# Every value product of an attention stage as two products of 64 rows, in two PSUM banks, added up by VectorE

## The chip, the cores and the metric

The kernel runs on one core of a Trainium2 chip. The metric is the device time of one execution in microseconds (us), the median of several runs. A profiled execution gives, beside its own time, a span: from its first to its last instruction.

The core's engines have short names in the profile: PE is TensorE's products (matmuls), PEld its loads of the stationary operand, DVE is VectorE, ACT is ScalarE, POOL is GpSimd, SP is SyncE, which here issues the DMA transfers. TensorE writes to PSUM, eight banks of 128 partitions x 512 f32 values; VectorE and ScalarE read them.

## The reference

```python
xn = layernorm(x)                                   # x: 2048 x 576
q, k, v = split(xn @ wqkv)                          # 32 heads of 18
p = softmax(q @ k.T * 18 ** -0.5)                   # 2048 x 2048 per head
s = (p @ v, heads joined) @ wo
g = silu((gelu(xn @ w_gate) * (xn @ w_up)) @ w_down)  # 4608 hidden values
out = x + s * g
```

## The kernel before, in words

After a prologue that normalizes x and computes q, k and v, the kernel runs attention and the feed-forward block side by side. Attention works on 32 units u (8 groups of four heads, times 4 blocks of 512 query tokens); a unit has 16 key tiles kt of 128 tokens. The feed-forward block works on sections of 128 hidden values for 512 tokens. The order on TensorE is written out by hand; the other engines' instructions are ordered by the scheduler, apart from those kept in program order.

`section` (L533) issues 27 pairs of products pg and pu (L413), one on the partitions 0 to 63 and one on 64 to 127, and mixes 16 further pairs in: of each, one is a score product pe (`score_mm`, L729) and one a product pm for a later unit's score maxima (`max_mm`, L698). Each pm takes a bank of tag m, of which there are three (`BANKS`), and VectorE reduces it to its row maxima (L699). Each pe takes a bank of tag s, and ScalarE makes the exponentials pT from it (L730). The pg and pu banks have tag f.

The loop at L829 goes through 128 attention sections, four per unit (i = 0 to 3). After every odd one it issues a value stage: `values` (L755) for eight key tiles. For each key tile and each of the four heads a, one product multiplies the values VS (128 key tokens x 32 columns, of which 19 count: ones for the softmax's sum and the 18 values) with the exponentials pT (128 key tokens x 512 queries). It accumulates over the eight key tiles in the partitions 32a to 32a + 31 of one bank acc of tag m. After the first stage of a unit ScalarE copies acc to the SBUF tile SUM (L767); after the second VectorE adds acc to SUM (L769), and DMAs store the sums (L772 and `store_sums`, L605). So 64 value stages alternate between the two kinds of eviction. VS and pT are f32, and the trace has two instructions per product.

After every even attention section `downs` (L573) issues the down products py (L465), 48 pairs of 64 rows x 288 columns in banks of the tags m, s and f, whose sums VectorE adds to Y (L453); VectorE also does the feed-forward's elementwise work (L427, L434, L440), and GpSimd the splits of weights and hidden values.

The section behind a value stage begins with a pair pg/pu; its first score pair comes second, and its first pm needs a bank of tag m again. Banks of a tag are handed out in turn.

Of the kernel before, what the change touches and what calls it, by code (L numbers as in the profile page):

```python
# [8 lines left out]
F32 = mybir.dt.float32  # L9
F32R = mybir.dt.float32r  # L10
AF = mybir.ActivationFunctionType
ALU = mybir.AluOpType
# [5 lines left out]
P = 128  # L18
NT = S // P
TB = 512  # L20
# [3 lines left out]
HR = 64  # L24
# [9 lines left out]
NA = NS // SLOTS  # L34
VC = NT // NA
VV = 2 * VC
KB, VB = 7, 2
# [32 lines left out]
def kernel(ctx: ExitStack, tc: tile.TileContext, x, wqkv, wo, w_gate, w_up, w_down, out):  # L70
    nc = tc.nc
# [85 lines left out]
    with tc.tile_pool(name="pro", bufs=1) as pro, tc.tile_pool(name="pps", bufs=1, space=PSUM) as pps:  # L157
# [45 lines left out]
        def norm(xr, b, between=None, behind=None):  # L203
            keep = tc.keep_in_program_order if b == 1 else lambda i: i
            st = pro.tile([P, 4, 8], F32, name="st", bufs=2)
            for j in range(4):
                bs = pro.tile([P, 2, 6], F32, name="bs", bufs=2)
                for h in range(2):
                    one = nc.vector.bn_stats(bs[:, h, :], xr[j][:, 288 * h:288 * h + 288])  # L209
                    keep(one)  # L210
                if behind and j == 0:
                    behind(one)
                nc.vector.bn_aggr(st[:, j, 0:2], bs)
            var, r, t = st[:, :, 1], st[:, :, 3], st[:, :, 4]
            nc.scalar.activation(t, var, AF.Sqrt, bias=eps)
            if between:
                between()
            nc.vector.reciprocal(r, t)
            nc.vector.scalar_tensor_tensor(t, r, -0.5, r, op0=ALU.mult, op1=ALU.mult)
            nc.vector.scalar_tensor_tensor(t, var, EPS, t, op0=ALU.add, op1=ALU.mult)  # L220
            nc.vector.scalar_tensor_tensor(r, t, 1.5, r, op0=ALU.add, op1=ALU.mult)
            for j in range(4):
                last = nc.vector.tensor_scalar(xr[j][:, 0:D], xr[j][:, 0:D], st[:, j, 0:1], st[:, j, 3:4],
                                               op0=ALU.subtract, op1=ALU.mult)
                nc.scalar.activation(xr[j][:, D:D + HR], xr[j][:, R0:D], AF.Copy)
            return last
# [42 lines left out]
        def split_qk(t, raw):  # L269
            hi, lo = (pro.tile([P, KT, P], F32R, name=f"q{m}{t}") for m in "hl")  # L270
            first = split(hi, lo, raw)
            put_qk(t, hi, lo)
            return first
# [62 lines left out]
        last = norm(xr, 0, first_hi, first_loads)  # L336
# [10 lines left out]
        for b in range(NB):  # L347
            for n, t in enumerate(ORDER):
                if n == (2 if b == 0 else 0) and b + 1 < NB:
                    xr = load_x(b + 1)  # L350
                if b == 0 and ahead_qk:
                    first = split_qk(*ahead_qk.pop(0))
# [34 lines left out]
    ps = ctx.enter_context(tc.tile_pool(name="ps", bufs=1, space=PSUM, reuse_waits="tile"))  # L387
# [213 lines left out]
    def store_sums(g, cols):  # L601

        for a in range(QD):
            h = QD * g + a
            kept(nc.sync.dma_start(oT[h * DH:(h + 1) * DH, cols], SUM[32 * a + 1:32 * a + 1 + DH, :]))  # L605
# [7 lines left out]
    def at(n, part, what, *args):  # L613
        todo.setdefault((n, part), []).append(lambda: what(*args))
# [10 lines left out]
    SUM = key.tile([P, TB], F32, name="accs")  # L625
# [19 lines left out]
    with tc.tile_pool(name="att", bufs=1, reuse_waits="tile") as att:  # L645
        VS = [att.tile([P, VC * VW + 32 - DH - 1], F32, name=f"VS{i}") for i in range(VB)]
# [28 lines left out]
        QS, MX, ACC, PT, DEN, PIECE = {}, {}, {}, {}, {}, {}  # L675
# [79 lines left out]
        def values(u, kt):  # L755
            j, g = divmod(u, NQ)
            first, last = kt % VV == 0, kt % VV == VV - 1
            if first:
                ACC[u] = ps.tile([P, TB], F32, name="acc", tag="m", bufs=3)
            pt = PT.pop((u, kt))  # L760
            for a in range(QD):
                c, t = divmod(kt, VC)
                v = t * VW + (DH + 1) * a
                nc.tensor.matmul(ACC[u][32 * a:32 * a + 32, :], VS[(u * NA + c) % VB][:, v:v + 32], pt[:, a, :],  # L764
                                 start=first, stop=last, skip_group_check=True)
            if last and kt < VV:
                nc.scalar.activation(SUM, ACC.pop(u), AF.Copy)  # L767
            elif last:
                nc.vector.tensor_tensor(SUM, ACC.pop(u), SUM, op=ALU.add)  # L769
            if kt == NT - 1 and u < NU - 1:  # L770
                cols = slice(j * TB, (j + 1) * TB)
                nc.sync.dma_start(sT[QD * g:QD * (g + 1), cols], SUM.rearrange("(a p) t -> a p t", p=32)[:, 0, :])  # L772
                store_sums(g, cols)
                rt = rT[QD * g:QD * (g + 1), cols]
                todo.setdefault(((u + 1) * NA, 0), []).insert(0, lambda: sums(u, rt))
                at((u + 1) * NA + 2, 2, reciprocals, u, rt)
                for h in range(2 if u < NU - 2 else 0):
                    at((u + 1) * NA + 3 + h, 2 * h, load_piece, u, h)
                    at((u + 1) * NA + 4 + h, 2 * h, norm_piece, u, h)
# [10 lines left out]
        def sums(u, rt):  # L790
            j, g = divmod(u, NQ)
            den = DEN[u] = att.tile([P, QD * TB // P], F32, name="sums", bufs=2)
            nc.sync.dma_start(den, sT[QD * g:QD * (g + 1), j * TB:(j + 1) * TB]
                              .rearrange("a (c s) -> a c s", s=QD * TB // P))
# [34 lines left out]
        for n in range(NU * NA):  # L829
            u, i = divmod(n, NA)  # L830
            s0 = n * SLOTS
            new_x = (FF["n"] + 1) % (NR * G) == 0
            if new_x:
                load_k(n - 1 + KB, behind_it)
            section([p for s in range(s0, s0 + SLOTS) for p in slot_pairs(s)])
            if n > 0 and not new_x:
                load_k(n - 1 + KB)
            if n > NU * NA - KB:
                load_wo((n - 1) % KB)
            if i == 1 and u + 2 < NU:  # L840
                load_q(u + 2)
            tasks(n, 0)
            um, im = divmod(s0 + LEAD + SLOTS, NS)
            if im == 0 and um <= NU:
                max_neg(um - 1)
                at(n + 1, 0, max_rows, um - 1)
            if i % 2:
                for kt in range((i - 1) * VC, (i + 1) * VC):
                    values(u, kt)
                load_v(n + 1)  # L850
                load_v(n + 2)
            downs()
            tasks(n, 2)
            finish()


    with tc.tile_pool(name="epi", bufs=1, reuse_waits="tile") as epi:
# [80 lines left out]
        for n in range(NU * NA, ENDS):  # L938
            first, last = n == NU * NA, n == ENDS - 1
# [102 lines left out]
```

## Time and profile before

| | |
|---|---|
| median of 3 runs | 2548.01 us (2547.96 to 2548.17) |
| the profiled execution | 2547.22 us |
| its span | 2545.4 us |
| granted TensorE clock | 1.000 |
| value products (L764), busy | 452.8 us, 4096 instructions |
| reduces of the maxima (L699), busy | 1249.6 us, 2048 instructions |
| exponentials (L730), busy | 1153.3 us, 2048 instructions |
| 1190.00 to 1223.25 us, two sections with a value and a down stage: DVE, ACT, POOL busy | 27.19, 22.96, 17.15 us of 33.25 |

A row of the timeline gives the start, the length, the engine, the line, the operation, output<-input, the shape (rows*columns of the stationary operand, then the moving operand), and how many instructions are merged in it (x4); in brackets the engine's idle time before it and what ended that. A product's length goes to the end of its last result, so products that follow each other overlap in the rows, and the distance of starts shows the pace. A row of groups ends with busy time in us, mean ns of one, idle time before, and what ended it. A row of waits has the total in us, how often, and the longest.

### The profile page before, as it was taken

What the parts mean: (1) busy time and instruction counts of PE and PEld (TensorE: products, weight loads), DVE (VectorE), ACT (ScalarE), POOL (GpSimd) and SP (SyncE); (2) the same over time, 40 slices, a digit from 0 to 9 for tenths busy, and PEclk for the clock granted to TensorE, in tenths of its full rate; (3) what the DMA queues carried; (4) which work ended last, traced back from release to release, by engine and by line L of the source; (5) the groups of instructions that cost most, each with busy time, mean ns of one, the idle gap of its engine ahead of it and who ended that gap; (6) DMA issues with size and microseconds to landing.
All of it is one profiled execution on the core that took longest, in us unless ns stands there. A gap on an engine that the chain in (4) does not pass through costs nothing.

```text
span 2545.4 us, 63167 instructions
## 1 busy us (share of the span) xinstructions
PE 2538.4 (100%) x23974; PEld 2008.4 (79%) x23974; DVE 1950.4 (77%) x3499; ACT 1555.1 (61%) x3050; POOL 1320.7 (52%) x1447
## 2 busy tenths in 40 slices
PE   9999999999999999999999999999999999999999
PEld 8888877777777777777777787777777777787798
DVE  5316988888888888888888888888888888887277
ACT  3223366666677666676666677666676666676612
POOL 2117545555465554445565545554446555455675
PEclk9999999999999999999999999999999999999999
DMA  8876444444465444444455444444446444444483
GB/s 267 269 241 158 100 103 106 100 111 109 107 150 121 104 109 112 113 112 110 111 125 140 116 111 106 105 108 112 109 109 153 115 109 109 108 106 99 114 242 107
DMA packets 398686, 325.51 MB, mean 128 GB/s; under 512 B 117408, under 2 KB 309184, under 8 KB 398384
## 3 DMA queue, kind: packets, MB, share of 16 engines
q1 hardware_dynamic: 398384, 321.47, 49.7%
q8 instruction: 191, 3.13, 0.5%
q14 instruction: 111, 0.91, 0.1%
HBM read 266.63 MB, written 54.70 MB: 126 GB/s over the span
## 4 chain that ended last, share of the span: by engine, by line
PE 98%; ACT 1%; DVE 0%; DMA 0%; SPq 0%; issue 0%; ACTq 0%
PE pg L413 29%; PE py L465 18%; PE acc L764 18%; PE pm L698 9%; PE pe L729 9%; PE po L180 7%; PE pu L413 6%; PE po L902 2%; ACT pT L730 1%; PE pt L241 0%; SPq L665 0%; DMA xx<-in_A_x_dram 0%; DVE bs L209 0%; ACT t L426 0%; DMA KS<-qk 0%
## 5 line engine op out<-in xcount | busy, mean ns | idle before, releaser
L730 ACT ACTIVATE pT<-pe 128x512 f32<-128x512 f32 x2048 | 1153.3, 598 | 368.7 <-PE pm L698 226.3
L699 DVE TENSOR_REDUCE mx<-pm 128x1 f32<-128x512 f32 x2048 | 1249.6, 680 | 151.3 <-PE pm L698 149.0
L413 PE MATMUL pg<-xd,wh 64*128 64x512 f32 x2592 | 928.9, 390 | 0.0
L413 PE MATMUL pu<-xd,wh 64*128 64x512 f32 x2592 | 928.6, 390 | 0.0
L698 PE MATMUL pm<-KS,q 64*128 64x512 f32 x2048 | 779.0, 388 | 0.8 <-DMA KS<-qk 0.5
L729 PE MATMUL pe<-q,KS 64*128 64x512 f32 x2048 | 775.2, 387 | 0.0
L413 PEld LDWEIGHTS pg<-xd,wh 64*128 64x128 f32 x2592 | 476.5, 184 | 115.9 <-POOL wh L106 21.1
L413 PE MATMUL pg<-xd,wl 64*128 64x512 f32 x1296 | 501.6, 387 | 0.0
L413 PE MATMUL pu<-xd,wl 64*128 64x512 f32 x1296 | 501.4, 387 | 0.0
L413 PEld LDWEIGHTS pu<-xd,wh 64*128 64x128 f32 x2592 | 477.0, 184 | 2.0
L764 PE MATMUL acc<-pT,VS 128*32 128x512 f32 x4096 | 452.8, 594 | 0.0
L108 POOL TENSOR_TENSOR wl<-raw,wh 128x384 fp32r<-128x384 f32 x432 | 434.2, 1019 | 13.7
L106 POOL TENSOR_SCALAR hh<-t 128x512 fp32r<-128x512 f32 x128 | 79.1, 618 | 652.0 <-DVE t L440 637.8
L698 PEld LDWEIGHTS pm<-KS,q 64*128 64x128 f32 x2048 | 374.2, 184 | 31.1 <-DVE mx L699 4.3
L729 PEld LDWEIGHTS pe<-q,KS 64*128 64x128 f32 x2048 | 370.9, 184 | 21.9
L465 PE MATMUL py<-dh,hh 64*128 64x288 f32 (+1 forms) x2160 | 360.3, 294 | 0.3
L465 PE MATMUL py<-dl,hh 64*128 64x288 f32 (+1 forms) x2160 | 358.7, 292 | 0.0
L465 PE MATMUL py<-dh,hl 64*128 64x288 f32 (+1 forms) x2160 | 358.3, 292 | 0.0
L764 PEld LDWEIGHTS acc<-pT,VS 128*32 128x32 f32 x4096 | 127.4, 110 | 289.9 <-issue 278.0
L106 POOL TENSOR_SCALAR wh<-raw 128x384 fp32r<-128x384 f32 x432 | 217.2, 515 | 143.7 <-PE pu L413 83.4
L453 DVE TENSOR_TENSOR Y<-py,Y 128x288 f32<-128x288 f32 x544 | 227.1, 452 | 59.8 <-PE py L465 52.7
L413 PEld LDWEIGHTS pg<-xd,wl 64*128 64x128 f32 x1296 | 238.7, 184 | 32.1
(119 smaller groups left out, 3106.7 us busy)
## 6 DMA issues: line engine op xcount, KB each, us to landing
KS<-qk SPq DMA_DIRECT2D x1536, 36.0 KB
raw<-in_B_w_gate_dram SPq DMA_DIRECT2D x144, 288.0 KB
raw<-in_B_w_up_dram SPq DMA_DIRECT2D x144, 288.0 KB
raw<-in_B_w_down_dram SPq DMA_DIRECT2D x67, 576.0 KB
VS<-vs SPq DMA_DIRECT2D x128, 152.0 KB
qk<-t SPq DMA_DIRECT2D x72, 256.0 KB
q<-qk SPq DMA_DIRECT2D x384, 36.0 KB
xx<-in_A_x_dram SPq DMA_DIRECT2D x32, 288.0 KB
```

The source lines that it names most:

```text
L106: first = nc.gpsimd.tensor_scalar(hi, raw, 1.0, 1.0, op0=ALU.mult, op1=ALU.mult)
L108: low_part[:] = [keep(nc.gpsimd.tensor_tensor(lo, raw, f(hi), op=ALU.subtract))]
L180: nc.tensor.matmul(o, st, m, start=(i == 0), stop=(i == len(terms) - 1))
L413: nc.tensor.matmul(o, w[1 + wp][k][rr, c, :], xd[xp][k][rr, c, :], start=(i == 0), stop=(i == len(terms) - 1))
L453: one = kept(nc.vector.tensor_tensor(yy, py, yy, op=ALU.add))
L465: return nc.tensor.matmul(py, hs[g][a][rr, j * P:(j + 1) * P], wd[w][rr, g, 288 * c:288 * c + 288], start=start, stop=stop)
L698: nc.tensor.matmul(pm, QS[u, r][rr, t * P:(t + 1) * P], KS[(u * NA + c) % KB][r][rr, :], start=True, stop=True)
L699: nc.vector.tensor_reduce(MX[u][:, 2 * r + a, t, c:c + 1], pm, axis=AX.X, op=ALU.max)
L729: nc.tensor.matmul(pe, KS[(u * NA + c) % KB][r][rr, t * P:(t + 1) * P], QS[u, r][rr, :], start=True, stop=True)
L730: nc.scalar.activation(PT[u, kt][:, 2 * r + a, :], pe, AF.Exp, scale=SCALE)
L764: nc.tensor.matmul(ACC[u][32 * a:32 * a + 32, :], VS[(u * NA + c) % VB][:, v:v + 32], pt[:, a, :], start=first, stop=last, skip_group_chec ...
L902: nc.tensor.matmul(po, parts_of(b, j)[x_][:, k, :], OW[w][c][k], start=(i == 0), stop=(i == len(OUT) - 1))
```

## The change

A value product is issued as two, one for each half of the 128 key tokens (partitions 0 to 63 and 64 to 127); the halves h accumulate in two banks acc of tag m, both held for the whole stage. At the end the first half is evicted as before (by ScalarE after a unit's first stage, by VectorE after its second), and the second half is added to SUM by VectorE.

```diff
             if first:
-                ACC[u] = ps.tile([P, TB], F32, name="acc", tag="m", bufs=3)
+                ACC[u] = [ps.tile([P, TB], F32, name="acc", tag="m", bufs=3) for h in range(2)]
             pt = PT.pop((u, kt))
             for a in range(QD):
                 c, t = divmod(kt, VC)
                 v = t * VW + (DH + 1) * a
-                nc.tensor.matmul(ACC[u][32 * a:32 * a + 32, :], VS[(u * NA + c) % VB][:, v:v + 32], pt[:, a, :],
-                                 start=first, stop=last, skip_group_check=True)
-            if last and kt < VV:
-                nc.scalar.activation(SUM, ACC.pop(u), AF.Copy)
-            elif last:
-                nc.vector.tensor_tensor(SUM, ACC.pop(u), SUM, op=ALU.add)
+                for h in range(2):
+                    rr = slice(HR * h, HR * h + HR)
+                    nc.tensor.matmul(ACC[u][h][32 * a:32 * a + 32, :], VS[(u * NA + c) % VB][rr, v:v + 32], pt[rr, a, :],
+                                     start=first, stop=last, skip_group_check=True)
+            if last:
+                for h, acc in enumerate(ACC.pop(u)):
+                    if h == 0 and kt < VV:
+                        nc.scalar.activation(SUM, acc, AF.Copy)
+                    else:
+                        nc.vector.tensor_tensor(SUM, acc, SUM, op=ALU.add)
```

## The prediction

> **What bounds the kernel now.** I read the busy times, the chain that ended last, TensorE's waits and the costliest groups.
>
> ```profile
> PE 2538.4 (100%) x23974; PEld 2008.4 (79%) x23974; DVE 1950.4 (77%) x3499; ACT 1555.1 (61%) x3050; POOL 1320.7 (52%) x1447
> PE 98%; ACT 1%; DVE 0%; DMA 0%; SPq 0%; issue 0%; ACTq 0%
> PE pm L698 <- DMA KS<-qk: 0.5, 1, 0.5
> L699 DVE TENSOR_REDUCE mx<-pm x2048: 625/679/693, 212.9 to 2336.4; 128x1 f32<-128x512 f32 x187
> L764 PE MATMUL acc<-pT,VS x4096: 592/592/618, 324.3 to 2417.0; 128*32 128x512 f32 x196
> ```
>
> TensorE (PE) is on the chain for 98% of the span, and the longest wait that is listed for its products from the first score product on is 0.5 us. So time is won or lost only by what TensorE streams, by what lies between two streams, and by new waits. The value products (L764) are 4096 instructions: 64 stages of 64, that is 8 key tiles, 4 heads, and two instructions per product (the tile is plain f32). VectorE (DVE) is 77% busy as an average, but that average misleads. Here are the stage that starts at 1190.70 and its loads:
>
> ```profile
> 1190.38 0.39 PE L413 MATMUL pu<-xd,wh 64*128 64x512 f32 x1
> 1190.70 0.64 PE L764 MATMUL acc<-pT,VS 128*32 128x512 f32 x4
> 1190.70 0.16 PEld L764 LDWEIGHTS acc<-pT,VS 128*32 128x32 f32 x8 [0.35 <-issue]
> 1191.15 0.13 PEld L764 LDWEIGHTS acc<-pT,VS 128*32 128x32 f32 x4 [0.30 <-issue]
> 1191.58 0.13 PEld L764 LDWEIGHTS acc<-pT,VS 128*32 128x32 f32 x4 [0.30 <-issue]
> 1196.73 1.04 PE L764 MATMUL acc<-pT,VS 128*32 128x512 f32 x8
> 1197.70 0.50 PE L413 MATMUL pg<-xd,wh 64*128 64x512 f32 x1
> 1198.04 0.39 PE L698 MATMUL pm<-KS,q 64*128 64x512 f32 x1
> 1198.27 0.39 PE L413 MATMUL pg<-xd,wl 64*128 64x512 f32 x1
> ```
>
> The reader is to see three things. Four value products, one per head in its own 32 columns, run side by side, and a round of four takes 0.43 us (1191.15 to 1191.58): 16 rounds, 6.88 us. Around the stage, pairs of 64-row products come every 0.23 us (1198.04 to 1198.27). And both ends cost extra. Entry: 1190.38 to 1191.15 is 0.77 where 0.23 + 0.43 would do, 0.11 too much. Exit: the last round starts near 1196.73 + 1.04 - 0.59 = 1197.18; from there to 1198.04 is 0.86, where 0.43 + 0.23 would do, 0.20 too much. Together 0.31 us per stage.
>
> VectorE's reduces of the score maxima come at the pace at which TensorE makes them:
>
> ```profile
> 1185.37 6.07 DVE L699 TENSOR_REDUCE mx<-pm 128x1 f32<-128x512 f32 x10
> 1219.33 5.46 DVE L699 TENSOR_REDUCE mx<-pm 128x1 f32<-128x512 f32 x9
> 1223.95 0.64 PE L764 MATMUL acc<-pT,VS 128*32 128x512 f32 x4
> 1215.20 1.22 DVE L699 TENSOR_REDUCE mx<-pm 128x1 f32<-128x512 f32 x2
> 1215.88 0.18 PEld L698 LDWEIGHTS pm<-KS,q 64*128 64x128 f32 x1
> ```
>
> Ten back to back take 6.07 us: one each (6.07 - 0.68)/9 = 0.60 us, so 16 of a section need 9.6 us, and its 43 pairs (27 for gate and up, 16 with scores) 43 x 0.226 = 9.7 us. VectorE has next to no slack there, and the three PSUM banks of tag m tie it to TensorE. The last two rows show how tightly: the first of the two reduces ends at 1215.20 + 0.63 = 1215.83 and the load that needs its bank starts at 1215.88, 0.05 us later.
>
> **The change part by part.**
>
> *Streams.* Each product becomes two of 64 rows: 128 instructions and 128 loads a stage instead of 64 and 64. Four column tiles side by side are shown above; two row tiles side by side are the pg/pu pairs. Both at once is in no row. If eight run side by side, and the length goes by the 512 columns of f32 and not by the rows, a round stays 0.43 us. The eight loads at 1190.70 start within 0.16 - 0.11 = 0.05 us, 7 ns apart; four more streams put the last one 0.03 us later, 64 x 0.03 = **+1.9 us**. Bounds: below, the 64-row products around the stage need 0.23 us per 512 columns, half of 0.43, so at most -0.20 x 16 x 64 = -205 us; above, the halves run one after the other, +6.88 x 64 = +440 us. I take the value next to the rows for four columns and two rows, no change of pace.
>
> *The two ends.* The change keeps 64 rows throughout, so only the columns differ from the neighbours'. Whether that saves the 0.31 us (64 x 0.31 = 20 us) is answered by the one place where the trace changes the columns alone, 128 rows before and after:
>
> ```profile
> 329.87 1.47 PE L764 MATMUL acc<-pT,VS 128*32 128x512 f32 x12
> 331.27 0.40 PE L465 MATMUL py<-dh,hh 128*128 128x288 f32 x1
> 331.51 0.30 PE L465 MATMUL py<-dl,hh 128*128 128x288 f32 x1
> 331.64 0.29 PE L465 MATMUL py<-dh,hl 128*128 128x288 f32 x1
> ```
>
> The last round starts at 329.87 + 1.47 - 0.59 = 330.75, ends its 0.43 at 331.18, and the next product comes at 331.27, 0.09 late; the one behind it after 0.24 where 0.13 is the pace. 0.20 us again, as at 1197.70, where rows and columns both change. I take **0**, and keep -20 us as the other end.
>
> *The second bank at the entry.* Tag m has three banks. The last three score products of a section hold them; before, acc took the oldest. Now the second instruction of the stage needs the bank of the last product but one. At 1190.70 the reduces end at 1185.37 + 6.07 = 1191.44, the last but one at 1190.84; with 0.05 for the release the load can start at 1190.89, 0.19 after 1190.70. At 1223.95: 1219.33 + 5.46 = 1224.79, 1224.19, 1224.24, so 0.29. These two kinds of stage alternate. Behind the waiting load stand all the stage's other products; I take it that they wait with it, so the stage ends that much later. The reduces end at 2336.4 and stages come every 33.25 us (1190.70 to 1223.95) from 324.3 on: 61 have this wait. 61 x 0.24 = **+14.6 us**. Nothing below 0 is to be had here; above, if TensorE stood still until the last reduce, 0.6 us more each, +37.
>
> *The second eviction at the exit.* There is one more add of 0.69 us on VectorE per stage, in front of the next section's 16 reduces.
>
> ```profile
> 1197.92 0.60 ACT L767 ACTIVATE accs<-acc 128x512 f32<-128x512 f32 x1 [4.84 <-DMA KS<-qk]
> 1198.50 3.87 DVE L699 TENSOR_REDUCE mx<-pm 128x1 f32<-128x512 f32 x6 [4.69 <-PE pm L698]
> 1199.21 0.18 PEld L698 LDWEIGHTS pm<-KS,q 64*128 64x128 f32 x1
> 1199.66 0.18 PEld L698 LDWEIGHTS pm<-KS,q 64*128 64x128 f32 x1
> 1231.17 0.69 DVE L769 TENSOR_TENSOR accs<-acc,accs 128x512 f32<-128x512 f32 x1 [4.14 <-PE acc L764]
> 1231.78 4.44 DVE L699 TENSOR_REDUCE mx<-pm 128x1 f32<-128x512 f32 x7
> 1232.91 0.18 PEld L698 LDWEIGHTS pm<-KS,q 64*128 64x128 f32 x1
> 1234.40 0.56 SPq L772 DMA_DIRECT2D sT<-accs  x1
> L453 DVE TENSOR_TENSOR Y<-py,Y 128x288 f32<-128x288 f32 x544 | 227.1, 452 | 59.8 <-PE py L465 52.7
> ```
>
> First kind: ScalarE (ACT) copies half 0 until 1198.52, the add starts at 1198.57, the reduces 0.61 later at 1199.18 instead of 1198.50. The fourth score product takes the bank of the first reduce, free at 1199.18 + 0.68 + 0.05 = 1199.91; its load stood at 1199.66: 0.25 late. Second kind: adds at 1231.17 and 1231.78, first reduce at 1232.39, bank free at 1233.12 against 1232.91: 0.21 late. VectorE runs no faster than TensorE in the section, so this isn't won back by TensorE; what is left of VectorE's own delay (some 0.4 us) goes into its waits for finished sums in the down products (L453: 52.7 us, 0.8 per stage). 61 x 0.23 = **+14.0 us**. The store of the sums (L772) stood at 1234.40, far behind the second add's end at 1232.47, so SyncE's queue hides its delay; without that cover what stands behind it there (the key and query loads) would go 0.6 us later, once in every second stage. Bounds: 0 if VectorE's slack took it all; if VectorE is given the first reduce ahead of the add in the first kind, the second bank comes free at 1199.11 + 0.69 + 0.05 = 1199.85, and its load (third score product, at 1199.21) is 0.64 late: 0.39 x 31 = 12 us more.
>
> *Sum.* 1.9 + 0 + 14.6 + 14.0 = 30.5 us. The profiled execution took 2547.2 us (span 2545.4), 0.8 under the median of 2548.0. 2548.0 + 30.5 = 2578.5; I say 2578.
>
> **The rivals.**
>
> *TensorE can't be fed.* 128 products and 128 loads in 6.88 us are one instruction in 27 ns. The densest run is that of the down products:
>
> ```profile
> 1208.50 0.30 PE L465 MATMUL py<-dl,hh 64*128 64x288 f32 x2
> 1208.64 0.29 PE L465 MATMUL py<-dh,hl 64*128 64x288 f32 x2
> ```
>
> Two products (and two loads) in 0.13 us, 66 ns per product. If that is a ceiling, a stage takes 128 x 0.066 = 8.4 us, 1.5 more, +98 us; with the exit's 14 it ends near 2660. Against it: 128-row products come every 0.13 us too (331.51 to 331.64) with half the instructions, so 0.13 is the stream's length and no limit of issue. [...] Chance 0.12 (2610 to 2680).
>
> *The halves take turns:* +440 us and up, near 3000. Against it, row pairs and column fours each run side by side. 0.05.
>
> *The ends are spared.* Decided where the tile changes: if 64 rows kept means nothing extra there, -20 us. It is faster only if the waits at the banks, 28.6 us by the rows, come to under half of that sum as well; otherwise the reduces, not the ends, set when the stage starts, and it falls back towards the forecast: 2558 if the saving comes off whole. 0.07 for 2525 to 2543, 0.06 for 2543 to 2553.
>
> *A 64-row f32 stream runs at the 64-row pace.* This is the case on the faster side in one mechanism: place L764, price up to -205 us, about 2370; it decides once a round falls by 0.03 us (16 x 0.03 outweighs 0.48 of waits). Against it: the neighbours are another number format (one instruction per product, not two). 0.04.
>
> **How the numbers follow.** Forecast 0.66, own range 2560 to 2592 (one of the two waits missing, or the ends spared and swallowed by the waits; the reduce ahead of the add). The range of 2548 to 2670 takes in that, half of the case within 0.2%, and nearly all of the feeding limit: 0.66 + 0.03 + 0.11 = 0.8. Under 0.2% (5 us) is no difference that a measurement can tell. Faster 0.11, same 0.06, slower 0.83.
>
> **What would show it.** Right: rounds of eight still 0.43 us apart; first value load still 0.3 us behind the last pair, the second 0.2 to 0.3 us later; 32 + 64 adds of 0.69 us; the reduces after a stage 0.6 to 0.7 us later; periods of 33.7 instead of 33.25. Wrong: rounds longer or shorter than 0.43, products evenly spaced instead of in eights, or a stage whose first two loads start together.

## The result and the profile after

The changed kernel takes 2584.1 us (median of 4 runs, 2583.7 to 2584.3) against 2548.0 of the kernel before: ratio 1.0142, 95% interval 1.013 to 1.0155. It is slower by 36 us, where 30.5 were forecast. The profiled execution's span went from 2545.4 to 2582.3 us, 36.9 more. From the profile's page (busy times, the chain, and two groups):

```profile
PE 2575.0 (100%) x28070; PEld 2205.1 (85%) x28070; DVE 1978.9 (77%) x3563; ACT 1566.4 (61%) x3050; POOL 1320.4 (51%) x1447
PE 98%; ACT 1%; DVE 1%; DMA 0%; SPq 0%; issue 0%; DVEq 0%; ACTq 0%
L766 PE MATMUL acc<-pT,VS 64*32 64x512 f32 x8192 | 468.6, 591 | 0.0
L773 DVE TENSOR_TENSOR accs<-acc,accs 128x512 f32<-128x512 f32 x96 | 66.4, 692 | 298.5 <-PE acc L766 139.2
```

The page hides the cause: TensorE is as "busy" as before. The waits, 0.1 to 0.3 us each, lie under products that are still in flight, and a product whose load comes late is listed longer (0.47 us against 0.39, in rows below). The trace has to be cut where the work changes. I cut each of the 63 periods from one value stage to the next at the starts of TensorE's rows: the first value product, the first pg behind it, the first down product, the first product behind the last down product. Sums over the 63 periods, in us:

| | before | after | difference |
|---|---|---|---|
| value stage, to the next pg | 441.3 | 457.0 | +15.6 |
| the section behind it | 609.1 | 623.1 | +13.9 |
| down products | 417.5 | 422.1 | +4.6 |
| the next section, to the next stage | 618.3 | 620.3 | +2.0 |
| sum | 2086.2 | 2122.4 | +36.2 |

The line between the last two parts is soft, because in some periods the next section's first products come among the last down products: cut at that section's first product, and not behind the last down product, the two differences are +5.6 and +1.1. Their sum stays.

**The stage's start.** The loads and the reduces at one stage in the changed kernel:

```profile
1240.06 0.13 PEld L766 LDWEIGHTS acc<-pT,VS 64*32 64x32 f32 x2 [0.35 <-DVE mx L699]
1240.36 0.27 PEld L766 LDWEIGHTS acc<-pT,VS 64*32 64x32 f32 x15 [0.16 <-DVE mx L699]
1240.81 0.24 PEld L766 LDWEIGHTS acc<-pT,VS 64*32 64x32 f32 x8 [0.19 <-issue]
1238.43 2.47 DVE L699 TENSOR_REDUCE mx<-pm 128x1 f32<-128x512 f32 x4
```

Two loads (head 0, half 0) start, and the next comes 0.30 us behind the first. The four reduces end at 1238.43 + 2.47 = 1240.90, the last but one at 1240.30, and the second half's load follows at 1240.36: it waits for the second bank. The rest wait behind it. In the other kind of stage the gap is 0.17 us; these are its loads, then its first and last products and what follows:

```profile
1206.27 0.14 PEld L766 LDWEIGHTS acc<-pT,VS 64*32 64x32 f32 x2 [0.35 <-issue]
1206.45 0.18 PEld L766 LDWEIGHTS acc<-pT,VS 64*32 64x32 f32 x14
...
1205.96 0.39 PE L413 MATMUL pu<-xd,wh 64*128 64x512 f32 x1
1206.28 1.69 PE L766 MATMUL acc<-pT,VS 64*32 64x512 f32 x24
...
1212.05 1.49 PE L766 MATMUL acc<-pT,VS 64*32 64x512 f32 x23
1213.47 0.49 PE L413 MATMUL pg<-xd,wh 64*128 64x512 f32 x1
1213.81 0.39 PE L698 MATMUL pm<-KS,q 64*128 64x512 f32 x1
```

The ends are what they were: 0.32 from the last pu to the first value product, 1213.47 - (1212.05 + 1.49 - 0.59) = 0.52 from the last one to pg, then 0.34 to the next pair. Keeping 64 rows saved nothing.

**Behind the stage.** VectorE, ScalarE and the loads of the score products, first behind a stage that ScalarE evicts, then behind one that VectorE evicts:

```profile
1213.65 0.60 ACT L771 ACTIVATE accs<-acc 128x512 f32<-128x512 f32 x1 [5.02 <-PE acc L766]
1214.28 0.69 DVE L773 TENSOR_TENSOR accs<-acc,accs 128x512 f32<-128x512 f32 x1 [4.92 <-ACT accs L771]
1214.89 2.48 DVE L699 TENSOR_REDUCE mx<-pm 128x1 f32<-128x512 f32 x4
1215.62 0.18 PEld L698 LDWEIGHTS pm<-KS,q 64*128 64x128 f32 x1 [0.23 <-DVE mx L699]
...
1247.55 1.49 DVE L773 TENSOR_TENSOR accs<-acc,accs 128x512 f32<-128x512 f32 x2 [4.41 <-PE acc L766]
1248.96 2.48 DVE L699 TENSOR_REDUCE mx<-pm 128x1 f32<-128x512 f32 x4
1249.69 0.18 PEld L698 LDWEIGHTS pm<-KS,q 64*128 64x128 f32 x1 [0.30 <-DVE mx L699]
```

The reduces start 1214.89 - 1213.47 = 1.42 us behind the first pg, where it was 1198.50 - 1197.70 = 0.80: 0.62 later. In the second kind the two adds to SUM take 1.49 and the reduces start 1248.96 - 1247.38 (the first pg there) = 1.58 behind, against 1231.78 - 1230.96 = 0.82: 0.76 later. Both times the fourth score product waits for the first reduce.

### The profile page after: what moved, and what is told of

Same layout as the page of the kernel before. It is cut to its first block, busy times and chain, and to the rows that moved or that the text cites. A ratio compares the mean times of both kernels' runs of the same rounds, so it can differ in the third digit from the quotient of the medians.

```text
span 2582.3 us, 71437 instructions
## 1 busy us (share of the span) xinstructions
PE 2575.0 (100%) x28070; PEld 2205.1 (85%) x28070; DVE 1978.9 (77%) x3563; ACT 1566.4 (61%) x3050; POOL 1320.4 (51%) x1447
## 4 chain that ended last, share of the span: by engine, by line
PE 98%; ACT 1%; DVE 1%; DMA 0%; SPq 0%; issue 0%; DVEq 0%; ACTq 0%
PE pg L413 25%; PE acc L766 18%; PE py L465 18%; PE pu L413 9%; PE pm L698 9%; PE pe L729 9%; PE po L180 7%; PE po L906 2%; ACT pT L730 1%; PE pt L241 0%; DVE mx L699 0%; DMA xx<-in_A_x_dram 0%; SPq L665 0%; ACT t L426 0%; DVE t L434 0%
## 5 line engine op out<-in xcount | busy, mean ns | idle before, releaser
L699 DVE TENSOR_REDUCE mx<-pm 128x1 f32<-128x512 f32 x2048 | 1235.3, 680 | 9.1 <-PE pm L698 8.6
L766 PE MATMUL acc<-pT,VS 64*32 64x512 f32 x8192 | 468.6, 591 | 0.0
L108 POOL TENSOR_TENSOR wl<-raw,wh 128x384 fp32r<-128x384 f32 x432 | 434.0, 1018 | 13.7
L766 PEld LDWEIGHTS acc<-pT,VS 64*32 64x32 f32 x8192 | 246.6, 107 | 186.5 <-issue 84.1
L465 PE MATMUL py<-dh,hh 64*128 64x288 f32 (+1 forms) x2160 | 395.8, 295 | 0.3
L465 PE MATMUL py<-dl,hh 64*128 64x288 f32 (+1 forms) x2160 | 390.7, 293 | 0.0
L465 PE MATMUL py<-dh,hl 64*128 64x288 f32 (+1 forms) x2160 | 387.8, 292 | 0.0
L773 DVE TENSOR_TENSOR accs<-acc,accs 128x512 f32<-128x512 f32 x96 | 66.4, 692 | 298.5 <-PE acc L766 139.2
L465 PEld LDWEIGHTS py<-dh,hh 64*128 64x128 f32 (+1 forms) x2160 | 273.1, 184 | 12.9 <-issue 5.8
```

What stands on the lines that cost most here:

```text
L108: low_part[:] = [keep(nc.gpsimd.tensor_tensor(lo, raw, f(hi), op=ALU.subtract))]
L465: return nc.tensor.matmul(py, hs[g][a][rr, j * P:(j + 1) * P], wd[w][rr, g, 288 * c:288 * c + 288], start=start, stop=stop)
L699: nc.vector.tensor_reduce(MX[u][:, 2 * r + a, t, c:c + 1], pm, axis=AX.X, op=ALU.max)
L766: nc.tensor.matmul(ACC[u][h][32 * a:32 * a + 32, :], VS[(u * NA + c) % VB][rr, v:v + 32], pt[rr, a, :], start=first, stop=last, skip_group ...
L773: nc.vector.tensor_tensor(SUM, acc, SUM, op=ALU.add)
```

## The experiments

Diffs are against the changed kernel, unless the text says otherwise. The runs of the kernel before beside them had medians of 2547.1 to 2547.7 us. The theory, which I call "banks": (a) the second bank makes the stage's start wait for one reduce more, (b) VectorE's extra add at the stage's end pushes the reduces back, and the 64 rows themselves cost and save nothing. The rivals: the rows cost it, or VectorE's added time as such.

**One half alone.** The loop over halves runs once, with one bank; the second half of the rows is left out.

```diff
-                ACC[u] = [ps.tile([P, TB], F32, name="acc", tag="m", bufs=3) for h in range(2)]
+                ACC[u] = [ps.tile([P, TB], F32, name="acc", tag="m", bufs=3)]
...
-                for h in range(2):
+                for h in range(1):
```

> Only the half of the key tokens on partitions 0 to 63 is multiplied (the other half is left out), into one bank with one eviction: 64 rows stay, the second bank and the second add go. Theory (banks): 64 rows cost nothing by themselves, the two ends still cost 0.31 us, so the time of the kernel before, 2548 (2545 to 2551), stage 6.48 us from first to last product. Rival (rows): the split into 64 rows costs the 16 us that the stages grew by, 2560 to 2570. Rival (ends spared by equal rows): 2528.

2546.8 us, ratio 0.9997 (0.9988 to 1.0007). Every value product has 64 rows, and each of the four parts, summed over all periods, is within 0.6 us of the kernel before. So 64 rows, on partitions 0 to 63 alone, cost nothing, and rows equal to the neighbours' don't spare the ends: that rival falls. It doesn't yet show eight streams side by side.

**Two banks, whole rows, key tiles in turn.** Each bank gets every second key tile, in products of 128 rows.

```diff
-                for h in range(2):
-                    rr = slice(HR * h, HR * h + HR)
...
+                nc.tensor.matmul(ACC[u][kt % 2][32 * a:32 * a + 32, :], VS[(u * NA + c) % VB][:, v:v + 32], pt[:, a, :],
+                                 start=kt % VV < 2, stop=kt % VV >= VV - 2, skip_group_check=True)
```

> Products of 128 rows as before, key tiles in turn into two banks, second bank added by VectorE as in the change. Theory (banks): nearly the changed kernel's time, 2576 to 2584, a little less since the second bank is first needed by the fifth product and not the second. Rival (rows): 2548 to 2568, as the rows are whole again.

2547.4 us, ratio 0.9999 (0.9989 to 1.0009): my expectation missed by 30 us, and taken by itself the number speaks for the rows. VectorE's rows at a stage's end in this kernel say why it isn't a test of them:

```profile
1230.26 0.69 DVE L771 TENSOR_TENSOR accs<-acc,accs 128x512 f32<-128x512 f32 x1 [3.20 <-PE acc L764]
1231.20 0.69 DVE L771 TENSOR_TENSOR accs<-acc,accs 128x512 f32<-128x512 f32 x1 [0.24 <-PE acc L764]
1231.81 1.33 DVE L699 TENSOR_REDUCE mx<-pm 128x1 f32<-128x512 f32 x2
```

The first bank is complete one key tile early (0.86 us) and is added while TensorE still streams; the second add stands where the only one stood before, and the reduces start at 1231.81 (1231.78 before). At the start the second bank is needed 0.86 us in, when its reduce is long done. I had changed when the banks are needed together with the rows. Its page has another lesson:

```profile
PE 2538.1 (100%) x23974; PEld 2001.6 (79%) x23974; DVE 1990.6 (78%) x3563; ACT 1556.3 (61%) x3050; POOL 1320.2 (52%) x1447
```

VectorE has 40 us more work than before (1950.4), and the kernel is no slower. The rival "VectorE's added time as such" falls.

**The same, mended.** Against the run just told: the heads are shifted against each other, so both banks are needed by the first products and complete with the last.

```diff
-                nc.tensor.matmul(ACC[u][kt % 2][32 * a:32 * a + 32, :], VS[(u * NA + c) % VB][:, v:v + 32], pt[:, a, :],
+                nc.tensor.matmul(ACC[u][(kt + a) % 2][32 * a:32 * a + 32, :], VS[(u * NA + c) % VB][:, v:v + 32], pt[:, a, :],
```

> Products of 128 rows, product (key tile kt, head a) into bank (kt + a) mod 2: the stage's second product needs the second bank and both banks are complete only with the last key tile, as in the change, but no product has 64 rows. It mends the run with the banks in turn, where the first bank was complete a key tile early and was evicted inside the stage. Theory (banks): the whole cost of the change without its 64 rows, 2580 to 2585. Rival (rows): 2548 to 2568.

2579.7 us, ratio 1.0125 (1.0109 to 1.0142), 0.3 under the range that "banks" expected (from 2580) and far from the rows' 2548 to 2568. The four parts: +13.7, +11.8, +4.7, +1.8. So 32 of the 36 us come without a single product of 64 rows. The other 4 are 2 in the stages and 2 in the sections behind them; there the second of the two adds to SUM starts 1.42 - 0.69 = 0.73 us behind the first (last row below) and not 0.80 as in the change, and why is open. The wait at a stage's start stands in its loads: two start, and the third comes at 1238.53, 0.27 us behind the first and just after the last reduce but one ends, at 1236.00 + 3.07 - 0.60 = 1238.47.

```profile
1236.00 3.07 DVE L699 TENSOR_REDUCE mx<-pm 128x1 f32<-128x512 f32 x5
1238.26 0.14 PEld L764 LDWEIGHTS acc<-pT,VS 128*32 128x32 f32 x2 [0.35 <-DVE mx L699]
1238.53 0.30 PEld L764 LDWEIGHTS acc<-pT,VS 128*32 128x32 f32 x7
1238.98 0.28 PEld L764 LDWEIGHTS acc<-pT,VS 128*32 128x32 f32 x4 [0.15 <-issue]
...
1245.70 1.42 DVE L771 TENSOR_TENSOR accs<-acc,accs 128x512 f32<-128x512 f32 x2 [4.36 <-PE acc L764]
```

**Two banks one after the other.** Key tiles 0 to 3 of a stage go to one bank, 4 to 7 to another, each evicted when complete. From the diff against the kernel before (a new bank is likewise taken at every fourth key tile):

```diff
...
+            if kt % (VV // 2) == VV // 2 - 1:
+                acc = ACC.pop(u)
+                if kt < VV // 2:
+                    nc.scalar.activation(SUM, acc, AF.Copy)
+                else:
+                    nc.vector.tensor_tensor(SUM, acc, SUM, op=ALU.add)
```

> 128 rows, two banks one after the other: the first four key tiles of a stage into the first, the last four into the second; as many evictions as in the change, but the first one falls in the middle of the stage and the second bank is needed only then. Theory (banks): both waits go although VectorE's work is that of the change, 2548 to 2552. Rival (VectorE's added time is what counts, wherever it stands): 2570 to 2584.

2547.9 us, ratio 1.0 (0.9991 to 1.001), as "banks" expected: as many evictions as in the change and no cost, as the extra one falls inside the stage.

**The change without the second add.** The second half's bank is filled but never added, so its share is missing from the sums.

```diff
-                for h, acc in enumerate(ACC.pop(u)):
-                    if h == 0 and kt < VV:
...
+                acc = ACC.pop(u)[0]
+                if kt < VV:
+                    nc.scalar.activation(SUM, acc, AF.Copy)
+                else:
+                    nc.vector.tensor_tensor(SUM, acc, SUM, op=ALU.add)
```

> The change with the second half's bank written but not evicted or added (that half is left out of the result): the wait at the entry stays, VectorE's extra add goes. Theory (banks, entry and exit apart): 2548 + 16 = 2564 (2561 to 2568): stages as long as in the change, the sections behind them as before. Rival (all from the extra add on VectorE): 2548. Rival (all from the second bank at the entry and its consequences): 2584.

2564.4 us, ratio 1.0065 (1.005 to 1.008), as expected. The stages cost +15.5 us, the other three parts together +0.8. So (a), with what the streams cost, is 16 us by itself, and all but 0.8 us of what comes behind the stage hangs on the second add.

**The second half added by GpSimd.** ScalarE copies it into a used tile of pT.

```diff
                     if h == 0 and kt < VV:
                         nc.scalar.activation(SUM, acc, AF.Copy)
+                    elif h == 0:
+                        nc.vector.tensor_tensor(SUM, acc, SUM, op=ALU.add)
                     else:
-                        nc.vector.tensor_tensor(SUM, acc, SUM, op=ALU.add)
+                        nc.scalar.activation(pt[:, 0, :], acc, AF.Copy)
+                        nc.gpsimd.tensor_tensor(SUM, pt[:, 0, :], SUM, op=ALU.add)
```

> The change with the second half copied by ScalarE and added by GpSimd: the second bank is still needed at the entry and evicted at the exit, but VectorE has no added work (in a unit's second stage ScalarE copies beside VectorE's add). Theory (banks at the entry, VectorE's delay at the exit): the entry's 16 us stay, most of the other 20 go, 2564 to 2570. Rival (the second bank being held at the exit is what counts): the bank comes free at much the same time, 2580 to 2584.

2565.4 us, ratio 1.0074 (1.0057 to 1.009): +15.8 at the stages, +2.4 behind them. Its rows behind a unit's first stage:

```profile
1205.29 0.60 ACT L771 ACTIVATE accs<-acc 128x512 f32<-128x512 f32 x1 [4.97 <-PE acc L766]
1205.79 0.59 ACT L775 ACTIVATE pT<-acc 128x512 f32<-128x512 f32 x1
1206.46 1.30 POOL L776 TENSOR_TENSOR accs<-pT,accs 128x512 f32<-128x512 f32 x1 [0.45 <-ACT pT L775]
1205.92 2.66 DVE L699 TENSOR_REDUCE mx<-pm 128x1 f32<-128x512 f32 x4 [4.87 <-PE pm L698]
```

The second bank is still held until 1206.38, 1.1 us behind the start of the first copy (1.3 in the change: 1214.28 + 0.69 - 1213.65), but VectorE goes straight to the reduces, and the sections behind such stages are as long as in the kernel before, where the change adds 0.13 us to each. So in this kind of stage it is VectorE's delay that costs, and not the bank's being held. Behind a unit's second stage the run doesn't separate the two: there ScalarE's copy runs beside VectorE's add, and both banks come free together (1239.55 and 1239.60 in one such stage). It would be the better way to sum the halves, but it stays 18 us over the kernel before.

**One bank, one more VectorE instruction.** The kernel before, with this behind each eviction:

```diff
+            if last:
+                nc.vector.tensor_tensor(SUM, SUM, SUM, op=ALU.max)
```

> The kernel before with one bank and 128 rows, and one more VectorE instruction of a tile of 128x512 behind each eviction, on SUM alone. Theory (VectorE's delay at the exit costs by itself): no wait at the entry, the section behind a stage and the down products grow as in the change, 2548 + 10 to 2548 + 22 (if an instruction on SBUF alone takes as long as one that reads PSUM; proportionally less if shorter). Rival (only the bank matters): 2548.

2576.4 us, ratio 1.0115 (1.010 to 1.013), +29 where 10 to 22 were expected. Nothing at the stages (0.0), +22.6, +4.1 and +2.8 behind them. On average the instruction is longer than I thought possible; its group, and then its rows behind one stage:

```profile
L771 DVE TENSOR_TENSOR accs<-accs 128x512 f32<-128x512 f32 x64 | 54.3, 848 | 152.1 <-ACT accs L767 108.4 <-DMA VS<-vs 23.8 <-DMA KS<-qk 9.5
```

```profile
1243.58 0.69 DVE L769 TENSOR_TENSOR accs<-acc,accs 128x512 f32<-128x512 f32 x1 [4.14 <-PE acc L764]
1244.31 0.90 DVE L771 TENSOR_TENSOR accs<-accs 128x512 f32<-128x512 f32 x1
1245.12 8.45 DVE L699 TENSOR_REDUCE mx<-pm 128x1 f32<-128x512 f32 x14
1245.85 0.18 PEld L698 LDWEIGHTS pm<-KS,q 64*128 64x128 f32 x1 [0.57 <-DVE mx L699]
```

It takes 848 ns on average, where the add that reads PSUM takes 692 (I had allowed for shorter only). Operands in SBUF do not by themselves make an instruction longer: the feed-forward's step L440 in the kernel before, 128x512 f32 with both operands in SBUF, took 678 to 1528 ns, half of the 138 up to 692. Its five above 700 ns all ran beside an instruction of GpSimd, but six of the shorter ones did too; what makes such an instruction long no run shows. The extra instruction costs more than the change's add, 22.6 against 13.9 us in the section behind the stage, and shows (b) with the sign and the place right and the size not comparable. What carries over: with one bank and 128 rows, an instruction ahead of the reduces also costs time in the down products and in the section behind them (4.1 and 2.8).

**A fourth bank of tag m,** in the kernel before and in the changed one. The bank is taken from tag s, and the tiles of tag m get bufs=4 (not shown).

```diff
-BANKS = {"f": 2, "m": 3, "s": 3}
+BANKS = {"f": 2, "m": 4, "s": 2}
...
-                            pys[k] = bank("mmsmfmss"[k])
+                            pys[k] = bank("mmmmfmss"[k])
```

> The kernel before with four banks of tag m and two of tag s (one of the down sums moved from s to m). The base for the next kernel. Scores have one bank less: 2548 to 2600.

> The change with four banks of tag m and two of tag s. Theory (banks): with a fourth bank the second half takes a bank that is already free and later maxima have one more to go to, so the difference to the kernel before with the same banks falls from 36 us to 0 to 8. Rival (rows, or VectorE's time): the difference stays 30 to 36.

2619.4 us (ratio 1.0283, 1.0268 to 1.0298) and 2620.6 (1.0288, 1.0272 to 1.0303): the change costs 1.2 us here instead of 36. But both are 72 us above the kernel before: the sections got 25.6 and 29.2 us longer in sum, some 0.4 us each, with the same 16 reduces, so VectorE has slack in them. I put that down to the bank that the other scores lost; no run separates it from the moved down sum. So that the second add costs nothing here says little of (b). The start is clean. The value stages sum to 441.3 us in the one kernel and 442.7 in the other, and the loads of a stage in the changed kernel with four banks wait for no reduce:

```profile
1259.33 0.18 PEld L766 LDWEIGHTS acc<-pT,VS 64*32 64x32 f32 x16 [0.36 <-issue]
1259.79 0.15 PEld L766 LDWEIGHTS acc<-pT,VS 64*32 64x32 f32 x8 [0.28 <-issue]
1260.21 0.15 PEld L766 LDWEIGHTS acc<-pT,VS 64*32 64x32 f32 x8 [0.28 <-issue]
1260.64 0.15 PEld L766 LDWEIGHTS acc<-pT,VS 64*32 64x32 f32 x8 [0.28 <-issue]
```

Eight loads come every 0.43 us, as four did before; the streams alone cost 1.4 us.

## Why the prediction was right, and where it was not

The forecast of +30.5 us stands against +36.2 in the parts of the trace (+36.1 in the medians). Its terms:

| term | forecast | measured |
|---|---|---|
| streams | +1.9 | +1.4 (with four banks, where no load waits); +2.0 (15.6 of the change less 13.7 of two banks mixed) |
| the two ends | 0 | 0 |
| second bank at the entry | +14.6 | +13.7 (two banks mixed, without 64 rows) to +14.2 (15.6 less 1.4) |
| second eviction at the exit, up to the down products | +14.0 | +13.9 |
| the same, in the down products and behind them | 0 | +6.6 |

*Streams: right.* Eight products run side by side, and a round of 64 rows takes the 0.43 us that one of 128 rows takes. The rival that TensorE can't be fed needs a ceiling, of 66 ns per product for its 2660 us and a lower one for the bottom of its range (2610); no run shows either: with four banks eight products come in 0.43 us, 54 ns each, each with its load. The halves don't take turns (+440 us), and f32 with 64 rows keeps its own 0.43 us, where the pairs of pg and pu come every 0.23.

*The two ends: right.* One half alone, with the rows of the neighbours, is no faster than 128 rows (2546.8). The gaps at start and end are unchanged.

*The entry: right in mechanism and size.* The two stages shown wait 0.30 and 0.17 us where 0.29 and 0.19 were worked out (the means of the two kinds, up to the last reduces, are 0.28 and 0.19), and all products behind the waiting load wait with it. Leaving out or moving the second add doesn't touch this (+15.5 and +15.8 with the streams in it); a fourth bank removes it.

*The exit: right in sum, by luck.* Two errors cancel. Behind a stage that ScalarE evicts, 0.25 us were forecast and 0.13 came; behind one that VectorE evicts, 0.21 and 0.33. In the first, the fourth score product in the kernel before and in the changed one, the load of the second being shown above (1215.62):

```profile
1199.88 0.39 PE L698 MATMUL pm<-KS,q 64*128 64x512 f32 x1
```

```profile
1215.66 0.47 PE L698 MATMUL pm<-KS,q 64*128 64x512 f32 x1
```

From one pg to the other are 1213.47 - 1197.70 = 15.77 us. The load would have stood at 1199.66 + 15.77 = 1215.43 and came 0.19 late; the product would have ended at 1200.27 + 15.77 = 1216.04 and ended at 1216.13, 0.09 late. By the first down product the delay is 1223.48 - 1213.47 = 10.01 against 1207.59 - 1197.70 = 9.89, so 0.12: some more is added in the pairs between. The load had stood 0.22 us ahead of its product (1199.66 and 1199.88) and now stood 0.04 ahead (1215.62 and 1215.66): part of the 0.22 is a cushion, which I hadn't counted. In the second kind the second add reads the SUM that the first writes. The two took 1.49 us, where 0.61 + 0.69 were forecast, so the reduces were 0.76 late and not 0.61.

*The failed step* is the sentence that what is left of VectorE's own delay "goes into its waits for finished sums in the down products". It priced at nothing what cost 6.6 us, more than the whole miss. VectorE did lose 5.7 us of these waits (L453: 52.7 before, 47.0 after), so the slack exists, but it is not where it was needed: VectorE waits for the later sums, and not ahead of the first one. VectorE's first sums in a down stage, before and after, and the loads there in the changed kernel:

```profile
1211.10 1.18 DVE L453 TENSOR_TENSOR Y<-py,Y 128x288 f32<-128x288 f32 x3
```

```profile
1223.48 0.32 PE L465 MATMUL py<-dh,hh 64*128 64x288 f32 x2
1227.21 1.18 DVE L453 TENSOR_TENSOR Y<-py,Y 128x288 f32<-128x288 f32 x3
1227.38 0.18 PEld L465 LDWEIGHTS py<-dh,hh 64*128 64x128 f32 x1
1227.72 0.18 PEld L465 LDWEIGHTS py<-dh,hh 64*128 64x128 f32 x1 [0.15 <-DVE Y L453]
```

The down products start at 1207.59 before and at 1223.48 after. The first sum follows 1211.10 - 1207.59 = 3.51 us behind, and 1227.21 - 1223.48 = 3.73 after: 0.22 us of the delay are left, and a down product waits 0.15 us for the bank. Where VectorE evicts the stage, the delay left is 0.06 (3.21 and 3.27 us), and the down stage cost 0.01 on average against 0.13 in the other kind. In both kinds VectorE comes out of the section's reduces some 0.2 us late; but in this one it used to stand idle for 0.29 us ahead of the feed-forward's first step (L427), and now does for 0.10:

```profile
1241.97 0.69 DVE L427 SCALAR_TENSOR_TENSOR t<-t,pg 128x512 f32<-128x512 f32 x1 [0.29 <-ACT t L426]
```

So in half of the stages the delay was won back, but ahead of the first sum and not in the waits that the prediction named.

The other runs say that this comes from the delay of the reduces: the down products' extra is absent where the reduces are on time (one half -0.6 us, two banks with whole rows in turn -0.3, no second add -0.1) and there where they are late (two banks mixed +4.7, the extra instruction +4.1). That the +2.0 us in the section behind (+1.1 by the other cut) have the same root I infer from the same runs (+1.8, +2.8; 0.4 or less in the three others); I haven't traced them to a row. GpSimd's version has +0.7 and +1.5 in these two parts without a further add on VectorE, which stays open.

## What to carry to other kernels

Price a second accumulator bank by two moments, not by busy time: when its first product needs the bank that someone else must still empty (13.7 to 14.2 us here), and where its eviction stands in the queue of the engine that TensorE depends on next (13.9 us, and 6.6 behind that). Where the banks filled one after the other, the early eviction fell inside the stage and cost nothing (2547.9 us against 2547.6), with as many evictions as in the change. And where a delayed engine is said to "win it back" in its waits, look whether those waits come before the next point at which it is needed.

## What the runs showed of the hardware that was not expected

With four banks of tag m, eight f32 streams of 64 rows by 32 columns ran side by side: eight products of 512 columns and their eight loads in 0.43 us, 54 ns each. Going from 64 by 128 to 64 by 32 and back left the gaps at the stage shown what they are with 128 by 32: 0.32 us from the last pu to the first value product, and 0.86 from the start of the last round to the second pair behind it (1212.95 to 1213.81, as 1197.18 to 1198.04). VectorE's extra instruction on 128x512 f32 with both operands in SBUF took 848 ns on average, and the step L440 with such operands from 678 to 1528 ns; the add with one operand in PSUM took 692. An add that reads what the add ahead of it wrote started 1.49 - 0.69 = 0.80 us behind it in the changed kernel and 0.73 with two banks mixed; a reduce that doesn't depend on the add started 0.61 behind. A weight load came 0.19 us late, and its product ended 0.09 late.
